# Two more batches' first layer in seven block products for eight, and 186 re-ranked operations, in a fused attention and MLP-mixer kernel

## The chip, the core and the metric

The kernel runs on one core of one Trainium2 chip. The core has five engines with queues of their own: PE (TensorE, the matmuls; the loading of its weights is shown as PEld), DVE (VectorE), ACT (ScalarE), POOL (GpSimd, which here issues most DMAs) and SP (SyncE, which issues DMA transposes and stores). Each engine works off its queue in the order in which the program was written; semaphores hold an instruction until what it needs is done. Matmuls write to PSUM, which has eight banks of 128 x 512 fp32 here; DVE and ACT empty it.

The metric is the device time of one execution in microseconds (us), the median of three runs.

## The reference

Eight batches, eight heads, 576 positions, head size 64. Attention with a sliding window of 128 and a linear bias (ALiBi), then an MLP mixer: a token-mixing pair of layers over the positions and a channel pair over the 512 features.

```
scores = q @ k^T / 8 ;  bias = -slope[h] * |i - j| ;  only 0 <= i - j < 128
x = softmax(scores + bias) @ v                    # heads side by side: 8 x 576 x 512
h = relu(x^T @ w_tok1) @ w_tok2                   # 576 -> 256 -> 576
u = x + h^T
out = u + relu(u @ w_ch1) @ w_ch2                 # 512 -> 1536 -> 512
```

## The kernel before, in words

**Tiles and stages.** Batches are taken in pairs: four blocks of 128 positions of each batch, and one tail block that holds the last 64 positions of both, so nine blocks to a pair. For each batch `main(b)` is the channel pair of layers and `side(b + 1)` the attention and the token mixing of the next batch. The two are interleaved on all engines. What `side` leaves for `main` is `ub` (the sum u, positions by features) and `uT` (its transpose, features by positions), which from batch 3 on is made by DMA transposes that SP issues (L974).

**The first layer.** A chunk (`chunk`, L1460) is four matmuls of 128 x 512 into one bank, 128 hidden units for the batch's 512 positions; one relu by ACT (L1466) or DVE (L1467) empties the bank into `r2`. Twelve chunks make a batch. In batch 7 (`UNITS[7]` is 3) the layer is cut into three units instead (`unit`). Each unit does the work of four chunks as a 2 x 2 block product with seven products in place of eight (Strassen's scheme in Winograd's form). `halves` (L1323) makes four differences of `uT` once, and `hidden_sums` (L688) made the sums of the weights long before. A product (L1360) is four matmuls of 128 x 256 into one bank, half a chunk. Three banks serve a unit. The bank `y` takes products 1, 6, 7 and 4 one after the other, `w` takes 5 and 3, `z` takes 2. After products 1, 5 and 6 the bank is copied out as fp32 (`keep`, L1375, into the ring `ob`, which outputs use too). After 2, 3 and 7 the bank and a kept copy are added into `r2` (`join`, L1384) and a relu in place follows (L1386 on DVE or L1388 on ACT); after 4 a relu empties the bank (L1411). A product that goes on in a bank waits for the eviction before it. Beside it `tail_piece` (L1503) does the first layer of the tail block.

**The second layer** is done in seven products in all batches (`second`, L1637), over sums of the hidden layer that DVE makes (`second_sums`, L1485) in two halves, with evictions by DVE (L1608) and stores (L1620). The tail block follows (L1548, L1555).

**The attention of a block** is `scores` (L770), an exp by ACT (L785), a product with the mask by DVE (L795), `values` (L858), a reciprocal (L871) and a scaling (L874) by DVE. The token mixing is L905, L915, a relu (L923 on ACT, L924 on DVE), L948, L944 and the sum into `ub` by DVE (L966).

**What sets the order.** All of this is first collected as operations with an engine, a cost, a rank and what they need. `Plan.run` then goes through them by a clock of its own: on each engine the operation that can start first is taken, and among those ready together the one with the lowest rank. `Plan.emit` writes the program in the order of the starts found. Operations are numbered (`o.n`) in order of creation. An operation's `after` is the earliest start that the clock allows it. Neither rank nor `after` puts a wait into the program: they change only the order on each engine's queue, and which buffer and which of two engines an operation gets. POOL's operations keep an order of their own (`order`). An operation with `other` may go to a second engine. PSUM banks are a ring: `ONE` is the four banks 4 to 7, `ANY` all eight; `gated` holds a unit's banks to `ONE` until the last scores of the next batch's side work have been placed.

The constants that the change touches, and the loop of the first layer that reads `UNITS`:

```
SEEDS = [0] * 9
UNITS = [0, 0, 0, 0, 0, 0, 0, 3]
...
if u >= NHT // 4 - UNITS[b]:
    rk = unit(b, u, rank, uT, tt, r2)
else:
    for t in (2 * u, 2 * u + 1, 6 + 2 * u, 7 + 2 * u):
        rk = chunk(t)
```

Of the kernel before, what the change touches and what calls it, by code (L numbers as in the profile page):

```python
# [71 lines left out]
class Plan:  # L72
# [59 lines left out]

    def run(self):
        ops = self.ops
        dice = [random.Random(x) for x in SEEDS]
        for o in ops:
            if SEEDS[o.part]:
# [241 lines left out]
GROUPS = (((0, 1, 2, 3), 250),)  # L379
UORDER = (1, 5, 2, 6, 3, 7, 4)  # L380
UNIT_RANK = 0
UNIT_LATE = False
SECOND_LATE = False
GATE = True
BANKS = 8
ALIKE = 0
UNITS = [0, 0, 0, 0, 0, 0, 0, 3]
FILL = 60000.0
START = 4300.0
LATE = (1500.0, 2790.0)  # L390
# [26 lines left out]
def kernel(  # L417
# [244 lines left out]
    def weight_sums():  # L662
        lo, hi = slice(0, HN), slice(HN, DM)
        for g in range(2):
            a, z = slice(3 * g, 3 * g + 3), slice(HK + 3 * g, HK + 3 * g + 3)
            got = []
            for i, x, y in ((0, WC2[:, a, hi], WC2[:, a, lo]), (1, WC2[:, z, hi], WT[:, 0, a, :]),
                            (2, WC2[:, z, hi], WC2[:, a, hi]), (3, WC2[:, z, lo], WT[:, 1, a, :])):
                def go(i=i, x=x, y=y, a=a):
                    dve_.tensor_tensor(out=WT[:, i, a, :], in0=x, in1=y, op=ALU.subtract)  # L670
                needs = [lc2[3 * g]] if i == 0 else [lc2[3 * g], lc2[HK + 3 * g]] + ([got[i // 2]] if i % 2 else [])
                got.append(plan.op("DVE", 154 + 3 * HN / 1.92, go, RANKT + i, needs=needs))
            lt.append(got)
# [3 lines left out]
    def hidden_sums():  # L677
        for u in range(NHT // 4):
            up, dn = slice(2 * u * P, 2 * (u + 1) * P), slice(DCH // 2 + 2 * u * P, DCH // 2 + 2 * (u + 1) * P)
            x, y = slice(0, NCB // 2), slice(NCB // 2, NCB)  # L680
            own = slice(2 * u * P, 2 * (u + 1) * P)
            got = []
            for i, f, a, z in ((0, ALU.add, WC1[:, x, dn], WC1[:, y, dn]),
                               (1, ALU.subtract, WS[:, 0, :, own], WC1[:, x, up]),
                               (3, ALU.subtract, WC1[:, y, up], WS[:, 1, :, own]),
                               (2, ALU.subtract, WC1[:, x, up], WC1[:, x, dn])):
                def go(i=i, f=f, a=a, z=z, own=own):
                    dve_.tensor_tensor(out=WS[:, i, :, own], in0=a, in1=z, op=f)  # L688
                needs = [lc1[x] for x in (2 * u, 2 * u + 1, 6 + 2 * u, 7 + 2 * u)]
                needs += [got[-1]] if i in (1, 3) else []  # L690
                got.append(plan.op("DVE", 154 + 2 * 2 * P / 1.92, go, RANKS + i, needs=needs, after=SUMS_AT))
            ls.append({1: got[0], 2: got[1], 4: got[2], 3: got[3]})
# [12 lines left out]
    weight_sums()  # L705
    if any(UNITS):
        hidden_sums()
# [621 lines left out]
    def unit(b, u, rank, uT, tt, r2):  # L1329
# [24 lines left out]
        def product(m, bk, more=(), new=True):  # L1354
            l, r, ws, ts = L[m]

            def go():
                for c in range(2):
                    for cb in range(2):
# [6 lines left out]
                         **({"makes": bk} if new else {"adds": bk}))  # L1366
            if UNIT_LATE and new:
                marks["wait"].append(op)
            return rk

        def half_of(x):
            return x().rearrange("p (c n) -> p c n", c=2)

        def keep(e, bk, rk):
            return plan.op("ACT", 600, lambda: act_.copy(out=e()[:, :], in_=bk()[:, :]), rk + UNIT_RANK, makes=e, uses=[bk],  # L1375
                           other=("DVE", 690, lambda: dve_.tensor_copy(out=e()[:, :], in_=bk()[:, :])))

        def mark(op, rows):
            for t in range(rows.start, rows.stop):
                r2.parts.setdefault(t, []).append(op)  # L1380

        def join(e, bk, rows, cols, rk):
            o = lambda: r2()[:, rows, cols]
            add = plan.op("DVE", 690, lambda: dve_.tensor_tensor(out=o(), in0=half_of(bk), in1=half_of(e), op=ALU.add),  # L1384
                          rk + UNIT_RANK, uses=[bk, e], part=(r2, ("sum", rows.start, cols.start)))
            mark(plan.op("DVE", RELU, lambda: dve_.tensor_scalar(out=o(), in0=o(), scalar1=0.0, scalar2=None, op0=ALU.max),  # L1386
# [47 lines left out]
    def main(b, rank):  # L1434
# [76 lines left out]

        if not UNITS[b]:
            turn_ = [0, 1, 2, 6, 7, 8, 3, 4, 5, 9, 10, 11] if quick else list(range(NHT))
# [6 lines left out]
        else:  # L1520
            tt = halves(b, rank, uT)
            for u in range(NHT // 4):
                if u >= NHT // 4 - UNITS[b]:
                    rk = unit(b, u, rank, uT, tt, r2)
# [205 lines left out]
```

## Time and profile before

| | us |
|---|---|
| median of three runs | 276.57 (276.26 to 276.59) |
| the profiled execution | 276.21 |
| its span, first to last instruction | 274.2 |
| PE busy (matmuls) | 267.9 |
| PEld busy (weight loads) | 182.2 |
| DVE busy | 209.4 |
| ACT busy | 136.9 |
| POOL busy | 114.3 |

How to read it: the span is what the profile shows of one execution, and some 2 us lie around it in the time of that execution. Matmuls are pipelined and their ends are modelled, so PE's busy time counts overlapping matmuls once, and a matmul shown with 0.27 us occupies PE for less when others follow. A row of the chain of waits gives a run of matmuls its true length. "Idle before" in a group of instructions is the time in which their engine stood still just ahead of them, with what ended it. Groups are by line, engine, operation and tile; "128x512 bf16<-128x512 f32" is output and input, partitions by elements. In the timeline a row is a start, a length, engine, line, operation and count.

### The profile page before, as it was taken

The numbers are of one execution on the slowest core, as the hardware profiler recorded it, in microseconds if no ns is written. First come the engines' busy times: TensorE is split into PE (matmuls) and PEld (weight loads), VectorE is DVE, ScalarE is ACT, GpSimd is POOL, SyncE is SP. The second block draws the span as 40 slices with busy tenths as digits, with TensorE's granted clock in tenths as the row PEclk, the third lists the DMA queues.
The fourth block names the chain that finished last, engine by engine and source line by source line (L and its number), as shares of the span: only waits on it lengthen the run. The fifth ranks groups of instructions, "written<-read, shape, count | busy, mean of one in ns | idle before, by whom it ended". The sixth has DMA issues, their size and how long they took to land.

```text
span 274.2 us, 7149 instructions
## 1 busy us (share of the span) xinstructions
PE 267.9 (98%) x2896; PEld 182.2 (66%) x2896; DVE 209.4 (76%) x482; ACT 136.9 (50%) x221; POOL 114.3 (42%) x146
## 2 busy tenths in 40 slices
PE   8989999999999999999999999999999999999994
PEld 5767566676686656585658656486658655489983
DVE  7987699977997479675968469684969469697972
ACT  6963795326871396207930097206940087205500
POOL 8979796830496009600890009700850410022000
PEclk9999999999999999999999999999999999999999
DMA  8999999999999999979999939989995810143014
GB/s 201 178 175 181 166 159 182 155 157 197 157 118 141 199 161 103 154 119 199 192 151 136 211 127 89 150 119 214 181 142 91 229 42 2 28 108 116 2 41 151
DMA packets 160336, 38.57 MB, mean 141 GB/s; under 512 B 146544, under 2 KB 159472, under 8 KB 160304
## 3 DMA queue, kind: packets, MB, share of 16 engines
q0 software_dynamic: 109968, 19.64, 90.2%
q1 hardware_dynamic: 49104, 17.70, 34.3%
q10 hardware_dynamic: 1232, 0.79, 1.0%
q8 instruction: 22, 0.36, 0.6%
q14 instruction: 10, 0.08, 0.1%
HBM read 35.85 MB, written 9.44 MB: 165 GB/s over the span
## 4 chain that ended last, share of the span: by engine, by line
PE 92%; DMA 4%; ACT 1%; issue 1%; POOL 0%; DVE 0%; POOLq 0%
PE ps L1637 27%; PE ps L1460 26%; PE ps L858 6%; PE ps L770 5%; PE ps L905 4%; PE ps L948 4%; PE ps L1503 4%; PE ps L1548 4%; PE ps L1360 3%; DMA W<-in_moe_w_tok_dram 2%; DMA v<-in_v_dram 2%; PE ps L1446 1%; PE ps L733 1%; PE ps L915 1%; PE ps L944 1%; PE ps L983 1%
## 5 line engine op out<-in xcount | busy, mean ns | idle before, releaser
L1466 ACT ACTIVATE r<-ps 128x512 bf16<-128x512 f32 x73 | 43.3, 600 | 76.1 <-PE ps L1460 68.9
L1460 PE MATMUL ps<-uT,WC 128*128 128x512 bf16 x324 | 78.7, 379 | 0.0
L579 POOL DMA_DIRECT2D v<-in_v_dram x36 | 30.6, 850 | 84.4 <-PE ps L858 81.8
L785 ACT ACTIVATE pe<-ps 128x1024 bf16<-128x1024 f32 (+1 forms) x56 | 50.9, 962 | 0.9 <-PE ps L770 0.8
L1460 PEld LDWEIGHTS <-WC 128*128 128x128 bf16 x324 | 29.1, 98 | 29.9 <-issue 1.1
L1637 PEld LDWEIGHTS <-r 128*128 128x128 bf16 x384 | 36.7, 98 | 6.7 <-issue 0.9
L579 POOL DMA_DIRECT2D qk<-in_q_dram x35 | 30.3, 869 | 4.0 <-DMA qkT<-qk 2.0
L579 POOL DMA_DIRECT2D qk<-in_k_dram x35 | 30.3, 871 | 3.7 <-DMA qk<-in_k_dram 1.3
L795 DVE TENSOR_TENSOR pe<-pe,mask 128x1024 bf16<-128x1024 bf16 (+1 forms) x48 | 30.4, 650 | 1.5 <-ACT pe L785 1.3
L1637 PEld LDWEIGHTS <-s 128*128 128x128 bf16 x288 | 27.7, 98 | 4.7 <-issue 1.0
L1637 PE MATMUL ps<-WC,r 128*128 128x256 bf16 x192 | 25.3, 273 | 0.0
L874 DVE TENSOR_TENSOR xb<-ps,rt 128x256 bf16<-128x256 f32 (+1 forms) x60 | 24.5, 419 | 0.7
L966 DVE TENSOR_TENSOR ub<-ps,xb 128x512 bf16<-128x512 f32 x32 | 19.8, 681 | 5.2 <-PE ps L948 5.2
L1637 PE MATMUL ps<-WT,r 128*128 128x256 bf16 x192 | 23.8, 273 | 0.0
L1637 PE MATMUL ps<-WT,s 128*128 128x256 bf16 x192 | 23.6, 273 | 0.0
L1608 DVE TENSOR_TENSOR raw<-ps,ub 128x512 f32<-128x512 f32 x27 | 18.2, 681 | 6.7 <-PE ps L1637 6.6
L858 PE MATMUL ps<-v,pe 128*128 128x65 bf16 (+1 forms) x480 | 21.9, 195 | 0.0
L858 PEld LDWEIGHTS <-pe 128*128 128x128 bf16 (+1 forms) x480 | 18.4, 99 | 5.2 <-DVE pe L795 1.1
L1620 POOL DMA_DIRECT2D out_dram<-raw x6 | 4.3, 718 | 37.0 <-DVE raw L1608 37.0
L770 PEld LDWEIGHTS <-qkT 64*128 64x128 bf16 x448 | 11.9, 94 | 8.9 <-issue 7.4
L1608 DVE TENSOR_TENSOR raw<-ps,raw 128x512 f32<-128x512 f32 x19 | 13.0, 688 | 5.9 <-PE ps L1637 5.9
L1467 DVE TENSOR_SCALAR r<-ps 128x512 bf16<-128x512 f32 x11 | 7.5, 686 | 11.1 <-PE ps L1460 8.9
(142 smaller groups left out, 400.0 us busy)
## 6 DMA issues: line engine op xcount, KB each, us to landing
out_dram<-raw SPq DMA_DIRECT2D x21, 256.0 KB, 3.5
qk<-in_q_dram POOLq DMA_DIRECT2D x30, 128.0 KB, 6.3
qk<-in_k_dram POOLq DMA_DIRECT2D x30, 128.0 KB, 6.1
v<-in_v_dram POOLq DMA_DIRECT2D x28, 128.0 KB, 6.1
WC<-in_moe_w_ch_dram POOLq DMA_DIRECT2D x8, 384.0 KB, 7.0
out_dram<-raw POOLq DMA_DIRECT2D x6, 256.0 KB, 3.4
v<-in_v_dram POOLq DMA_DIRECT2D x16, 64.0 KB, 4.8
out_dram<-ob SPq DMA_DIRECT2D x3, 256.0 KB, 2.7
```

Source lines behind the costliest of these rows:

```text
L579: nc.gpsimd.dma_start(out=to()[p0 : p0 + n, :, :], in_=rows(src, b, s0, n))
L770: pe_.matmul(wide(e)[:, i, kind, a:z], lhsT=ts[kb]()[e * D : (e + 1) * D, NHP + i, :], rhs=ts[blk]()[e * D : (e + 1) * D, i, a:z], start=T ...
L785: act_.activation(out=pb()[:, e, :, lo:, c0:c1_], in_=wide(e)[:, :, lo:, c0:c1_], func=ACT.Exp, scale=scale)
L795: dve_.tensor_tensor(out=o, in0=o, in1=heads(mk, es), op=ALU.mult)
L858: pe_.matmul(view()[a:z, at, i, :], lhsT=pb()[:, e, i, kind, a:z], rhs=vb()[:, h, 0 : D + 1], start=m == 0, stop=m == len(mms) - 1, skip_g ...
L874: dve_.tensor_tensor(out=x4(), in0=view()[r0:r1_, :, :, 0:D], in1=rt()[r0:r1_, 0:n, :, :].broadcast_to([r1_ - r0, n, 4, D]), op=ALU.mult)
L905: pe_.matmul(t1[j]()[:, :], lhsT=W1[:, blk % NC, j * P : (j + 1) * P], rhs=xb()[:, blk, :], start=c == 0, stop=False)
L966: plan.op("DVE", 690, lambda blk=blk, ht=ht, hs=hs: dve_.tensor_tensor(out=ub()[:, blk, :], in0=ht()[:, hs], in1=xb()[:, blk, :], op=ALU.a ...
L1460: pe_.matmul(ct()[:, :], lhsT=WC1[:, cb, t * P : (t + 1) * P], rhs=uT()[:, cb, :], start=cb == 0, stop=cb == NCB - 1)
L1466: plan.op("ACT", 600, lambda t=t, ct=ct: act_.activation(out=r2()[:, t, :], in_=ct()[:, :], func=ACT.Relu), rk, part=(r2, t), uses=[ct], o ...
L1608: dve_.tensor_tensor(out=v, in0=bk().rearrange("p (c n) -> p c n", c=2), in1=src, op=ALU.add)
L1637: pe_.matmul(bk()[:, c * HN : (c + 1) * HN], lhsT=l(t, c), rhs=w(t), start=first, stop=g == 1 and t == HK - 1, skip_group_check=True)
```

## The change

`UNITS` gets a 3 for batches 3 and 5, as batch 7 has it: all three units of their first layers are made of seven products instead of four chunks. Batches 3 and 5 are the second ones of their pairs, with a tail block, and the attention of batches 4 and 6 runs beside them. This adds 31 operations to each of the two batches, so later numbers in the order of creation move by 31 and then 62, to 1463 operations in all.

Before the plan runs, a new table `NUDGES` adds a number to the rank of 186 operations and gives 108 of them a floor for their start on the planner's clock, in nanoseconds. 89 of them are on PE, 59 on DVE, 23 on ACT, 13 on SP and 2 on POOL; 58 stand in the opening and the first two batches. Operation 274 is the copy of the last quarter of batch 0's `uT` (L1252); 908 is a DMA transpose of batch 4's `ub` (L974); 1457 is the second quarter of the very last output piece (L1548). Of the table the first and the last line are shown, and one from the part of batch 3.

```diff
     def run(self):
         ops = self.ops
+        for item in NUDGES.split():
+            n, rank, after = item.split(":")
+            ops[int(n)].rank += float(rank)
+            ops[int(n)].after = max(ops[int(n)].after, float(after))
         dice = [random.Random(x) for x in SEEDS]
...
 UNIT_RANK = 0
+NUDGES = ("12:-413:10740 15:-584:0 94:12660:106875 180:-624:7624 186:-377:7996 192:249:0 200:-876:14352 203:991:11015 "
...
+          "761:-670:131162 763:-1726:129980 765:3407:134943 766:4821:138150 769:7217:135329 771:-17678:0 778:12399:0 "
...
+          "1424:-8640:0 1428:8959:0 1429:6857:0 1442:11650:0 1457:8055:268226 ")
 UNIT_LATE = False
...
-UNITS = [0, 0, 0, 0, 0, 0, 0, 3]
+UNITS = [0, 0, 0, 3, 0, 3, 0, 3]
```

The lines with the operations that the prediction names:

```diff
+          "247:-100:16202 250:-701:21012 258:-958:22351 264:1004:21827 274:-158:26502 277:5057:33779 285:2619:27844 "
...
+          "859:12978:132589 861:-3784:131883 868:-6245:133680 885:-2813:0 889:3606:0 894:2453:0 908:8907:151484 "
```

21 rows, old and new, of the table NUDGES are left out of this document.

## The prediction

> **What bounds the kernel now.** I read the page's shares first, then the chain of work that ended last, then a table of busy time by stretch. In the last, each row is a stretch, its length, and then the busy time of PE, PEld, DVE, ACT and POOL with instruction counts, the granted clock, the DMA share and GB/s.
>
> ```profile
> PE 267.9 (98%) x2896; PEld 182.2 (66%) x2896; DVE 209.4 (76%) x482; ACT 136.9 (50%) x221; POOL 114.3 (42%) x146
> ...
> PE 92%; DMA 4%; ACT 1%; issue 1%; POOL 0%; DVE 0%; POOLq 0%
> ```
>
> ```profile
> 0.00:30.00 30.00, 27.41 (x416) 20.06 (x416) 24.16 (x77) 19.37 (x36) 26.22 (x38) 1.00 1.56 184
> 30.00:112.00 82.00, 82.00 (x895) 52.85 (x894) 67.57 (x155) 49.48 (x83) 44.73 (x55) 1.00 1.71 157
> ...
> 121.00:145.00 24.00, 24.00 (x279) 14.60 (x277) 16.51 (x39) 15.20 (x22) 13.68 (x16) 1.00 1.58 175
> 145.00:156.00 11.00, 11.00 (x94) 8.81 (x92) 6.96 (x12) 0.60 (x1) 0.00 (x0) 1.00 1.56 190
> ...
> 183.50:207.60 24.10, 24.10 (x280) 14.70 (x278) 16.75 (x39) 15.20 (x22) 9.27 (x11) 1.00 1.49 167
> 207.60:219.00 11.40, 11.40 (x94) 8.87 (x92) 7.02 (x13) 0.60 (x1) 2.88 (x4) 1.00 0.67 175
> ```
>
> From 30 us on PE is busy in every stretch without a gap, at full clock, and the chain that ends last lies on it for 92%. The first layer of batch 3 fills 121 to 145 us together with the attention of batch 4; its second layer follows to 156. Batch 5 has the same picture at 183.5 and 207.6. So PE sets the pace, and in the dense part a new order alone has nothing to win: there is no PE idle time to remove. It can only lose. Only less PE work, or a better opening, can shorten the kernel.
>
> **The PE work that goes.** Two rows of the chain of waits (start, length, what) give both forms, a run of eight first-layer matmuls (two chunks, L1460) and a run of 28 half-width matmuls (seven products, L1360) in batch 7:
>
> ```profile
> 129.55 1.73 PE ps L1460 x8
> ...
> 249.98 3.06 PE ps L1360 x28
> ```
>
> A chunk is 1.73/2 = 0.865 us, twelve are 10.38 us. Three units of seven products are 3 x 3.06 = 9.18 us. Each changed batch loses 1.20 us of PE time, both together 2.40 us. Since PE has no gaps there, all of it counts, unless a wait takes its place.
>
> **The vector work that comes.** The groups of batch 7's first layer and of batch 3's as it is (busy, mean ns of one):
>
> ```profile
> L1384 DVE TENSOR_TENSOR r<-ps,raw 128x512 bf16<-128x512 f32 x8 | 5.5, 690 | 1.2 <-PE ps L1360 1.0
> L1375 ACT COPY raw<-ps 128x512 f32<-128x512 f32 x8 | 4.5, 586 | 11.4 <-PE ps L1360 11.4
> L1386 DVE TENSOR_SCALAR r<-r 128x512 bf16<-128x512 bf16 x8 | 2.4, 294 | 0.3
> L1411 ACT ACTIVATE r<-ps 128x512 bf16<-128x512 f32 x3 | 1.8, 597 | 2.1 <-PE ps L1360 2.1
> L1388 ACT ACTIVATE r<-r 128x512 bf16<-128x512 bf16 x1 | 0.6, 622 | 0.0
> L1323 DVE TENSOR_TENSOR tt<-uT x2: 411/412/414, 243.7 to 244.1; 128x512 bf16<-128x512 bf16 x2
> L1323 DVE TENSOR_TENSOR tt<-uT,tt x2: 416/416/416, 244.4 to 245.6; 128x512 bf16<-128x512 bf16 x2
> ```
>
> ```profile
> L1466 ACT ACTIVATE r<-ps 128x512 bf16<-128x512 f32 x11 | 6.5, 599 | 15.4 <-PE ps L1460 12.1 <-DVE xt L898 3.3
> ...
> 126.68 0.69 DVE L1467 TENSOR_SCALAR r<-ps 128x512 bf16<-128x512 f32 x1 [2.56 <-PE ps L1460]
> ```
>
> A batch has twelve chunk evictions now, eleven on ACT and one on DVE. In their place come 9 keeps (ACT), 9 joins that add a bank and a kept copy (DVE), 9 relus after them (DVE, or ACT at 0.622), 3 last relus (ACT) and 4 differences of the transposed input (DVE). For DVE in batch 3's stretch: 16.51 - 0.69 + 9 x 0.690 + 9 x 0.294 + 2 x 0.412 + 2 x 0.416 = 26.34 us, in a stretch that is to last 24.00 - 1.20 = 22.80 us. That is 3.54 us too much. ACT: 15.20 - 11 x 0.599 + 9 x 0.586 + 3 x 0.597 = 15.67 us, so 7.13 us are idle. If ACT takes all nine relus (5.60 us), DVE has 26.34 - 2.65 = 23.69 us and is still 0.89 us short. For batch 5 (16.75 in 24.10) the same sums give 3.68 and 1.03 us.
>
> What is short in the stretch must be worked off in the next, where DVE has 11.00 - 6.96 = 4.04 us idle (batch 5: 4.38). That hides it only if what is put off is not what PE wants next. PE wants two things next: the sums of the hidden layer (L1485), which stand behind the joins in DVE's queue, and the token mixing of the next batch (L905, L948), which stands behind that batch's masks and norms. The exposed part lies between 0 (all of it put off into idle time) and 3.54 + 3.68 = 7.22 us (none). I take the shortage that is left after the best split of the two engines, 0.89 + 1.03 = **1.92 us**: it is nearest to a schedule that uses the free ACT, and both engines would still be 98% busy, which queues worked off in order hardly beat.
>
> A sentence of the Trainium skill speaks against this change: "TensorEngine Tiling (Array Packing)", section "PSUM Bottleneck", says that a faster TensorE does not make the emptying of PSUM faster, so that the copies may become the bottleneck, and that both ScalarE and VectorE should do them. It speaks of another way to speed up TensorE, but the 24 instructions above that come for 12 have that shape; read strictly it would give the time of the vector rival below.
>
> **The waits that come.** In a unit one bank takes products 1, 6, 7 and 4 in turn, and each but the first waits for the eviction of the one before: behind the waiting matmul stands all of PE's queue. In batch 7 nothing competes on DVE; in batches 3 and 5 a join can stand behind a mask or two norms of the next batch:
>
> ```profile
> L795 DVE TENSOR_TENSOR pe<-pe,mask 128x1024 bf16<-128x1024 bf16 x6 | 4.0, 683 | 0.0
> ...
> L874 DVE TENSOR_TENSOR xb<-ps,rt 128x256 bf16<-128x256 f32 x8 | 3.4, 420 | 0.1
> ```
>
> One such step late costs PE 0.42 to 0.68 us unless another batch's matmuls are put between; that is a part of the 1.92, not beside it. Until the last scores of the side work have gone out, the units' banks are held to the four that the values, tail pieces and transposes use too.
>
> **The re-ranked operations.** By creation order 89 are PE's, 59 DVE's, 23 ACT's, 13 SP's and 2 POOL's. A floor (third number) shapes the order that is written out, and the chip does not wait for it. POOL keeps its own order, so the two loads stay where they are. On SP transposes and stores change places:
>
> ```profile
> 143.75 5.71 SPq L974 DMA_TRANSPOSE uT<-ub  x4
> ...
> 206.17 5.12 SPq L974 DMA_TRANSPOSE uT<-ub  x4
> ```
>
> ```profile
> uT<-ub SPq DMA_TRANSPOSE x20, 2.4
> ```
>
> ```profile
> 156.29 0.86 PE ps L1460 x4
> ...
> 218.71 0.86 PE ps L1460 x4
> ```
>
> Batch 4's four transposes are issued by 149.46, the last lands 2.4 us later at about 151.9, and the first layer that needs them starts at 156.29: 4.4 us to spare (batch 6: 213.7 against 218.71, 5.0). That is the cover for a token mixing that is put off; with PE 1.20 us earlier, 3.2 to 3.8 us are left.
>
> In the opening DVE makes the last quarter of the first transposed input just ahead of the matmuls that need it, and PE has a gap shortly before:
>
> ```profile
> 26.32 0.42 DVE L1252 COPY uT<-ps 128x512 bf16<-128x512 bf16 x1 [0.38 <-PE ps L1249]
> ```
>
> ```profile
> 17.43 0.67 PE L1178 MATMUL ps<-v,pe 128*64 128x65 bf16 x16 [0.47 <-ACT pe L1072]
> ...
> 26.12 1.24 PE L1446 MATMUL ps<-uT,WC 128*128 128x512 bf16 x5
> ```
>
> That copy (operation 274) is among the re-ranked, with a floor. One instruction of its size let in ahead of it costs 0.42 us; a better order could close the 0.47 us gap. Ends -0.47 and +0.42; I take +0.21, half of the loss, since the floors on this part put things back rather than forward.
>
> **The sum.** The profiled execution took 276.21 us (span 274.2, 2.0 around it). 276.21 - 2.40 + 1.92 + 0.21 = 275.94. The three runs' median, 276.57, lies 0.36 above the profiled one, so 276.30 on its scale. **Forecast: 276.3 us**, no change that can be told: a measurement tells 0.2%, here 276.02 to 277.12, from none. With every unknown at its good end it is 276.57 - 2.40 - 0.47 = 273.7, at its bad end 276.57 - 2.40 + 7.22 + 0.42 = 281.8.
>
> **Rivals.**
> B1, the gain stays: shortage wholly put off into the idle DVE time of the second layers. For it: 4.04 and 4.38 us are more than 3.54 and 3.68, and ACT stands idle for 10 us there. Against: the sums must come first. 276.57 - 2.40 + 0.21 = 274.4 us.
> B2, half of it stays, one batch hides and the other does not: 276.57 - 2.40 + 0.96 + 0.21 = 275.3 us.
> C, slower: DVE becomes the bound in the two stretches. Place: the joins' queue. As in batch 7, DVE keeps eight relus of nine, so it is 3.54 - 0.29 + 3.68 - 0.29 = 6.64 us short; the second layers, where it is idle 37% of the time, take 37% of that, and 63%, 4.18 us, stop PE. 276.57 - 2.40 + 4.18 + 0.21 = 278.6 us. It decides once more than 1.1 us a batch is exposed. For it: 26 us of work in 23; against: ACT's 7.13 idle us.
> D, the next batch's transposed input comes late: the mixing of batch 4 is what is put off, and one of its transposes has a floor of 151.484 where the trace issues the first at 143.75. If that one alone goes last, its 5.71/4 = 1.43 us and 2.4 to land end at 155.3, against 155.1 wanted: 0.2 us. If all four follow it, 151.5 + 5.71 + 2.4 = 159.6, 4.5 us late. Middle 2.3: 276.57 - 2.40 + 2.3 + 0.21 = 276.7 us.
> E, PE was not the bound, so nothing is won: then 276.57 plus the opening's 0.42 = 277.0 us. The full rows of PE and the chain's 92% speak against it. The Trainium skill, "Perfetto Trace Analysis", section "Identifying the Most-Contended Engine", would have it so: it says that matmul busy time misleads and weight-load busy time is the better measure. Here that is 66%, below DVE's 76%; the trace's chain does not agree.
>
> **How the numbers follow.** A 0.28 (of it 0.03 faster, 0.22 same, 0.03 slower), B1 0.20, B2 0.13, C 0.22, D 0.10 (half same, half slower), E 0.07 (0.03 same, 0.04 slower). A is the forecast, its own range 275.8 to 277.3. Faster: 0.03 + 0.20 + 0.13 = 0.36; same: 0.22 + 0.05 + 0.03 = 0.30; slower: 0.03 + 0.22 + 0.05 + 0.04 = 0.34. The range reaches from just under B1 to C, 274.3 to 278.6, and leaves out some 0.08 below and 0.10 above.
>
> **What would show it.** PE's matmul time on L1460 falls by 24 chunks and L1360 rises to 252 matmuls with 7 in 3.06 us; if not, the first term is wrong. The rows of the two first-layer stretches should show DVE above 95% busy and PE, for the first time after 30 us, with gaps before L1360 or L1637 released by DVE, near 2 us in all. No gaps there means B1; gaps of 4 us or more, C; a gap before batch 4's or 6's first L1460 released by the transposes, D. The last uT copy of the opening should start within half a microsecond of 26.32. Wrong altogether would be gaps in stretches whose work is unchanged.

## The result and the profile after

The changed kernel takes 275.53 us (median of 22 runs, 274.17 to 278.4) against 276.71 us for the kernel before (22 runs, 276.11 to 277.74): a ratio of 0.9955, 95% interval 0.9941 to 0.997. It is faster by 0.45%, 1.2 us, half of the 2.4 us of PE work taken out. The prediction said 276.3 us and no change that can be told. Executions far above the others of their kernel (278.4 us here, one in e2, two each in e8 and e10, one in e11) count in the medians given below but not in the ratios and intervals, and the profiles of e2 and e11 are of such executions; without them the medians of e2, e8, e10 and e11 are 276.36, 275.64, 275.64 and 275.41 us.

Line numbers: behind L384 a line of the kernel before stands 30 lines further down in the changed kernel (L1360 is L1390, L1384 is L1414), and 5 lines further down in the variants that keep only a part of the table.

The page of the changed kernel, the shares and the chain that ended last:

```profile
PE 264.7 (96%) x2939; PEld 189.7 (69%) x2969; DVE 222.4 (81%) x514; ACT 142.9 (52%) x221; POOL 114.6 (42%) x146
...
PE 85%; DMA 5%; issue 2%; ACT 2%; POOL 2%; DVE 2%; POOLq 0%; ACTq 0%
```

This execution took 276.43 us (span 274.6), 0.9 above its kernel's median, and 30 matmul records are missing in it. The same kernel was profiled twice more; run e10 (275.62 us, span 273.9) lies near the median and has all 2969 matmuls, so the stretches and groups are shown from there. Busy time by stretch (columns as in the prediction):

```profile
30.00:112.00 82.00, 81.27 (x886) 52.24 (x881) 67.15 (x156) 49.24 (x75) 44.17 (x54) 1.00 1.73 156
...
121.00:145.00 24.00, 23.72 (x326) 19.12 (x324) 22.84 (x55) 17.72 (x27) 13.31 (x16) 1.00 1.50 170
145.00:156.00 11.00, 11.00 (x81) 7.68 (x80) 8.52 (x15) 1.04 (x3) 0.33 (x1) 1.00 1.51 171
...
183.50:207.60 24.10, 24.10 (x329) 19.46 (x328) 23.13 (x56) 16.86 (x25) 9.27 (x11) 1.00 1.43 165
...
247.00:260.00 13.00, 12.52 (x127) 11.06 (x125) 10.55 (x23) 9.76 (x18) 1.32 (x2) 1.00 0.22 75
```

DVE is busy for 22.84 of 24.00 and 23.13 of 24.10 us in the two stretches of the changed first layers, 95 and 96%, as predicted. PE, however, stands still there for only 0.28 us in the first and not at all in the second. Most of the 0.28 is this wait in PE's timeline, for a transpose of queries and keys and not for DVE:

```profile
124.33 0.23 PE L800 MATMUL ps<-qkT 64*128 64x128 bf16 x2 [0.24 <-DMA qkT<-qk]
```

The larger gaps are in stretches whose work is unchanged: 0.48 us from 247 to 260 us, batch 7, and 0.73 us from 30 to 112 us, of which 0.43 are a wait for a load of batch 1's keys and 0.29 one for a reciprocal by DVE.

The groups of the first layer by line (busy, mean ns, idle before), e10 again:

```profile
L1490 PE MATMUL ps<-uT,WC 128*128 128x512 bf16 x228 | 55.0, 379 | 0.0
...
L1414 DVE TENSOR_TENSOR r<-ps,raw 128x512 bf16<-128x512 f32 x25 | 16.8, 683 | 1.7 <-PE ps L1390 1.1 <-ACT raw L1405 0.4
L1390 PE MATMUL ps<-tt,WS 128*128 128x256 bf16 x108 | 15.9, 273 | 0.0
...
L1390 PE MATMUL ps<-uT,WC 128*128 128x256 bf16 x72 | 10.3, 273 | 0.0
...
L1418 ACT ACTIVATE r<-r 128x512 bf16<-128x512 bf16 x11 | 6.8, 633 | 3.2 <-DVE r L1414 3.2
L1390 PE MATMUL ps<-uT,WS 128*128 128x256 bf16 x36 | 5.4, 272 | 0.5 <-ACT raw L1405 0.2 <-DVE raw L1406 0.2
L1390 PE MATMUL ps<-tt,WC 128*128 128x256 bf16 x36 | 5.4, 272 | 0.0
L1416 DVE TENSOR_SCALAR r<-r 128x512 bf16<-128x512 bf16 x16 | 5.3, 332 | 0.2
```

The products are 108 + 72 + 36 + 36 = 252 matmuls, the chunks 228, as forecast. Of the 27 relus behind the joins ACT takes 11 and DVE 16.

**Where PE's time goes, by stretch.** Idle time alone does not show it, since PE also gets slower between its matmuls. So this is worked out from the traces: at each time, the time gone less the work of all matmuls started by then, each line's matmul at its usual spacing in the kernel before. What this lost time is above that of the profiled execution of before, in us, by the stretch in which it arises. Most traces lack some 30 matmul records, so a cell is good to about 0.2 us (0.3 in the first column):

| kernel (run) | 0-60 | 60-120 | 120-150 | 150-180 | 180-215 | 215-245 | 245-258 | all |
|---|---|---|---|---|---|---|---|---|
| changed, first profile | 1.38 | -0.11 | 0.34 | 0.10 | 0.33 | 0.00 | 0.82 | 2.86 |
| changed (e4) | 0.08 | 0.00 | 0.35 | 0.09 | 0.22 | 0.10 | 1.01 | 1.84 |
| changed (e10) | 0.25 | 0.00 | 0.65 | 0.04 | 0.21 | 0.15 | 0.81 | 2.11 |
| units without the table (e1) | 0.97 | 0.00 | 1.19 | 0.00 | 1.73 | 0.00 | 0.00 | 3.90 |
| the same, 18 relus left out (e7) | 3.05 | -0.12 | 1.08 | 0.00 | 2.09 | 0.00 | 0.00 | 6.11 |
| changed, 18 relus left out (e8) | -0.25 | 0.00 | 0.08 | 0.11 | 0.22 | -0.01 | 0.90 | 1.05 |
| table without batch 7 (e3) | 1.95 | 0.00 | 0.35 | 0.09 | 0.23 | 0.10 | 0.05 | 2.78 |
| the same again (e9) | -0.02 | 0.00 | 0.58 | 0.01 | 0.22 | 0.10 | 0.98 | 1.86 |
| table's middle alone (e6) | 2.58 | 0.16 | 1.62 | -0.42 | 1.14 | 0.00 | 0.00 | 5.09 |
| before with the early entries (e5) | -0.25 | 0.00 | 0.27 | 0.00 | 0.00 | 0.00 | 0.00 | 0.01 |
| before, other stores (e12) | 0.70 | 0.00 | 0.00 | 0.00 | 0.51 | 0.00 | 0.00 | 1.21 |

The units kernels have 2.42 us less work in the same reckoning, so e10's last matmul should start 2.42 - 2.11 = 0.31 us earlier than before's; it starts at 269.90 against 270.27, 0.37 earlier. Three things are to be seen. The two changed first layers (120-150 and 180-215) lose 0.57 and 0.86 us with the table (e4 and e10) and 2.92 us without it (e1). Batch 7 loses 0.8 to 1.0 in five of the six profiles with the early and middle entries, all but e3's. And the opening differs by more than 1 us between executions of one and the same order.

### The profile page after: what moved, and what is told of

The parts are those of the page before. It is cut to its first block, busy times and chain, and to the rows that moved or that the text cites. A ratio compares the mean times of both kernels' runs of the same rounds, so it can differ in the third digit from the quotient of the medians.

```text
span 274.6 us, 7275 instructions
## 1 busy us (share of the span) xinstructions
PE 264.7 (96%) x2939; PEld 189.7 (69%) x2969; DVE 222.4 (81%) x514; ACT 142.9 (52%) x221; POOL 114.6 (42%) x146
## 4 chain that ended last, share of the span: by engine, by line
PE 85%; DMA 5%; issue 2%; ACT 2%; POOL 2%; DVE 2%; POOLq 0%; ACTq 0%
PE ps L1667 27%; PE ps L1490 16%; PE ps L1390 9%; PE ps L888 6%; PE ps L800 5%; PE ps L978 4%; PE ps L935 4%; PE ps L1578 4%; DMA qk<-in_k_dram 3%; PE ps L1533 3%; DMA out_dram<-raw 2%; PE ps L1725 1%; PE ps L1051 1%; PE ps L945 1%; PE ps L1077 1%
## 5 line engine op out<-in xcount | busy, mean ns | idle before, releaser
L1490 PE MATMUL ps<-uT,WC 128*128 128x512 bf16 x212 | 53.5, 379 | 0.8 <-issue 0.2
L1496 ACT ACTIVATE r<-ps 128x512 bf16<-128x512 f32 x55 | 32.2, 600 | 34.4 <-PE ps L1490 32.5
L1490 PEld LDWEIGHTS <-WC 128*128 128x128 bf16 x228 | 20.5, 98 | 20.2 <-issue 0.2
L1405 ACT COPY raw<-ps 128x512 f32<-128x512 f32 x23 | 13.1, 593 | 27.0 <-PE ps L1390 26.0
L904 DVE TENSOR_TENSOR xb<-ps,rt 128x256 bf16<-128x256 f32 (+1 forms) x63 | 25.6, 416 | 0.7
L1667 PE MATMUL ps<-WT,s 128*128 128x256 bf16 x192 | 24.9, 273 | 0.0
L888 PEld LDWEIGHTS <-pe 128*128 128x128 bf16 (+1 forms) x480 | 19.9, 99 | 6.6 <-issue 0.6
L888 PE MATMUL ps<-v,pe 128*128 128x65 bf16 (+1 forms) x480 | 23.4, 194 | 0.5 <-DVE rt L901 0.3
L1638 DVE TENSOR_TENSOR raw<-ps,raw 128x512 f32<-128x512 f32 x20 | 13.7, 686 | 6.2 <-PE ps L1667 6.0
L1414 DVE TENSOR_TENSOR r<-ps,raw 128x512 bf16<-128x512 f32 x25 | 16.7, 682 | 1.7 <-PE ps L1390 1.1
```

The source lines that it names most:

```text
L888: pe_.matmul(view()[a:z, at, i, :], lhsT=pb()[:, e, i, kind, a:z], rhs=vb()[:, h, 0 : D + 1], start=m == 0, stop=m == len(mms) - 1, skip_g ...
L904: dve_.tensor_tensor(out=x4(), in0=view()[r0:r1_, :, :, 0:D], in1=rt()[r0:r1_, 0:n, :, :].broadcast_to([r1_ - r0, n, 4, D]), op=ALU.mult)
L1490: pe_.matmul(ct()[:, :], lhsT=WC1[:, cb, t * P : (t + 1) * P], rhs=uT()[:, cb, :], start=cb == 0, stop=cb == NCB - 1)
L1496: plan.op("ACT", 600, lambda t=t, ct=ct: act_.activation(out=r2()[:, t, :], in_=ct()[:, :], func=ACT.Relu), rk, part=(r2, t), uses=[ct], o ...
L1638: dve_.tensor_tensor(out=v, in0=bk().rearrange("p (c n) -> p c n", c=2), in1=src, op=ALU.add)
L1667: pe_.matmul(bk()[:, c * HN : (c + 1) * HN], lhsT=l(t, c), rhs=w(t), start=first, stop=g == 1 and t == HK - 1, skip_group_check=True)
```

## The experiments

### Units and table apart

e1 is the change of `UNITS` alone, no table. e2 is the changed kernel without the 57 entries with numbers below 602, which lie in the opening and the first two batches, e3 without those of batch 7 (1354 and above). e5 is the kernel before with the 57 early entries alone; e6 has the units and the entries from 602 to 1353.

```diff
-UNITS = [0, 0, 0, 0, 0, 0, 0, 3]
+UNITS = [0, 0, 0, 3, 0, 3, 0, 3]
```

> The units in batches 3 and 5 without the table of ranks and floors. Theory 1 (the vector work of the units is nearly hidden; the changed kernel loses about 1.3 us elsewhere, in the opening and at batch 7's first units): the opening and the end stay as before, so most of the 2.40 us is seen, about 274.8 us. Theory 2 (the prediction's: the vector shortage in the two stretches costs about 1.9 us, and the table only moves it): 276.2 to 277.5 us, with PE gaps released by DVE inside the two first layers.

> The changed kernel without the 57 entries of the table for operations below 602 (opening and first two batches). Theory 1: the opening is that of before and the transposes of batch 1's q and k do not wait for their loads, about 1 us less than the changed kernel, 274.5 us. Theory 2: the opening's entries cost nothing, the waits there are scatter of the loads, 275.5 us as with the whole table.

> The changed kernel without the entries for batch 7's main part (operations from 1354 on). Theory 1, the part about batch 7: if the order there makes the kept copies wait for output stores, the wait of about 1 us goes and the time is 274.5 us; if the wait comes from batch 6 ending earlier against the same stores, it stays and the time is 275.5 us. Theory 2: 275.5 us.

> The kernel before with the 57 early entries of the table alone (operations below 602), no new units. If the early entries are worth what the run without them lacked against the whole table (about 1 us): 275.8 us against 276.8. If that difference was scatter of the opening's loads: 276.8 us, no change.

> Units in 3, 5 and 7 with the entries 602 to 1353 alone: neither the early ones nor batch 7's. If only the middle matters: 275.2 us, as without batch 7's entries. If the early entries are worth 1 us: 276.2 us.

| run | median us | ratio to before | interval |
|---|---|---|---|
| e1, units alone | 277.42 | 1.0036 | 1.0015 to 1.0057 |
| e2, no early entries | 276.52 | 0.9985 | 0.9957 to 1.0014 |
| e3, no entries of batch 7 | 275.19 | 0.9943 | 0.992 to 0.9966 |
| e5, early entries alone | 276.73 | 1.0005 | 0.9979 to 1.0031 |
| e6, middle alone | 276.71 | 0.9987 | 0.9956 to 1.0019 |

The units alone make the kernel slower, though they take 2.4 us of work from the engine that bounds it; with the table they make it faster, and the intervals are apart (e4 below is the changed kernel in e1's session: 0.9939 to 0.9988). The table's early entries without the units do nothing; its other entries were not run without the units. What the units lose without it, the chain of e1 shows (start, length, what), in batch 3:

```profile
131.45 0.65 PE ps L770 x16
132.10 1.93 ACT pe L785 x2
134.02 1.04 ACT r L1388 x2
135.06 0.50 ACT r2t L1508
...
135.60 0.40 PE ps L858 x8
```

and the timeline of PE, with the waits in brackets:

```profile
133.74 1.05 PE L1503 MATMUL ps<-uTt,WC 128*128 128x128 bf16 x16 [0.19 <-DVE r L1384]
135.60 0.40 PE L858 MATMUL ps<-v,pe 128*128 128x65 bf16 x8 [0.24 <-ACT r2t L1508]
```

PE waits for banks: values (L858) and the tail piece (L1503) want one of the four banks that the unit shares with them, and a join (L1384) or the tail's relu (L1508) has yet to empty it. Those stand in their engines' queues behind two exps (L785) and two relus (L1388). The same rows come again at 196 to 198.5 us. In e10's timeline of these stretches no wait of PE on a join, a relu or an exp reaches 0.15 us. That is not for want of vector work. The two stretches in e1 (PE, PEld, DVE, ACT, POOL as above):

```profile
121.00:145.00 24.00, 23.26 (x313) 18.43 (x314) 22.17 (x52) 20.37 (x39) 13.08 (x16) 1.00 1.41 159
...
183.50:207.60 24.10, 22.98 (x309) 18.10 (x310) 22.08 (x52) 20.16 (x38) 9.25 (x11) 1.00 1.49 164
```

DVE is busy for 22.17 and 22.08 us, less than with the table (22.84 and 23.13), and PE stands still for 0.74 and 1.12 us. What differs is the order. Which entries do it, those of PE's own queue or those of DVE and ACT, no run separates.

e6 shows a second kind. From its chain of waits in batch 3:

```profile
119.91 4.30 DMA uT<-ub
```

and PE's timeline there:

```profile
125.41 1.47 PE L1642 MATMUL ps<-WT,r 128*128 128x256 bf16 x12 [1.12 <-DVE raw L1613]
```

and DVE's:

```profile
124.33 0.43 DVE L1328 TENSOR_TENSOR tt<-uT 128x512 bf16<-128x512 bf16 x1 [1.82 <-DMA uT<-ub]
124.67 0.68 DVE L1613 TENSOR_TENSOR raw<-ps,raw 128x512 f32<-128x512 f32 x1
```

The differences (`halves`, L1328 here) stand at the head of DVE's queue and wait for a transpose that takes 4.30 us to land. Behind them stands an eviction of batch 2's second layer (L1613) that PE waits for. DVE is not short of time there, it stands idle for 1.82 us in front of the first difference, and PE loses 1.12 us. In e10 the same eviction stands ahead of the differences (DVE's timeline):

```profile
120.73 0.69 DVE L1638 TENSOR_TENSOR raw<-ps,raw 128x512 f32<-128x512 f32 x1 [0.72 <-PE ps L1667]
121.82 0.43 DVE L1353 TENSOR_TENSOR tt<-uT 128x512 bf16<-128x512 bf16 x1 [0.39 <-DMA uT<-ub]
```

With the units in, the early entries seem to be worth 0.3 to 0.4% (e2 against the changed kernel, e6 against e3), but the intervals of both pairs overlap. The table of lost time shows a place: e6 loses 2.76 us in the two first layers, e3, with the same entries for the middle and the early ones besides, 0.58. Without the early entries the planner reaches batch 3 by another path and writes another order there. That is one profile of each; how much of it the times hold stays open.

### Are the relus the shortage?

e7 is e1, and e8 the changed kernel, with the 18 relus behind the joins of batches 3 and 5 left out, so part of the hidden layer keeps its negative values and the time is that of 18 vector instructions less. The queues are the same otherwise.

```diff
-    lambda: dve_.tensor_scalar(out=o(), in0=o(), scalar1=0.0, scalar2=None, op0=ALU.max)
+    lambda: b == B - 1 and dve_.tensor_scalar(out=o(), in0=o(), scalar1=0.0, scalar2=None, op0=ALU.max)
...
-    other=("ACT", 600, lambda: act_.activation(out=o(), in_=o(), func=ACT.Relu))
+    other=("ACT", 600, lambda: b == B - 1 and act_.activation(out=o(), in_=o(), func=ACT.Relu))
```

> The units without the table, and the 18 relus after the joins of batches 3 and 5 left out (the order of all else is unchanged, the output is not the reference's). Theory 2 in the form that the first runs leave (without the table the vector queues hold PE up, some 1.2 us in batch 3 and 1.7 us in batch 5): with the relus gone from ACT's and DVE's queues at least 2 of these 2.9 us go, 277.4 to about 275.2 us, and the ACT relus vanish from the chain at 132 to 136 us. Rival: PE waits for the four banks that the units hold, whatever the vector engines do, and the time stays at 277 us or more.

> The changed kernel with the same 18 relus left out (the order of all else is unchanged, the output is not the reference's). If the table has already hidden the vector work, little is left to win: 275.5 to 274.9 us, at most 0.7 us. If a shortage near the predicted 1.92 us is still exposed: 273.7 us.

e7 takes 277.3 us (1.0026, 1.0 to 1.0053), e8 275.93 us (0.9957, 0.9933 to 0.9981): neither can be told from its twin with the relus. A shortage of vector time would have shrunk by the 18 relus (in e1 ten on DVE and eight on ACT), each at least 0.20 us from start to start (rows further down), 3.6 us of one engine or the other; but e7's two first layers lose 3.17 us of PE time against 2.92 in e1. The chain of e7 says why:

```profile
132.77 0.60 DVE pe L795
...
133.46 0.67 DVE pe L795
134.13 0.33 DVE xb L874
134.46 1.21 DVE r L1384 x2
...
135.71 1.07 PE ps L1503 x16
```

The two joins that free the banks (L1384) still stand behind two masks and a norm of the next batch. The queue's order sets the wait, and taking the relus out of it did not bring these joins forward enough. The rival of e7's expectation, that PE waits for the four shared banks whatever the vector engines do, fits its time too. e10 speaks against "whatever": with the same four banks and more work on DVE it loses 0.86 us where e1 loses 2.92. No run gave the units more banks. In e8 the two first layers lose 0.30 us against 0.57 and 0.86 in e4 and e10, so 0.3 to 0.6 us seem to hang on the relus once the order is right, below what the times can tell.

### The 0.8 to 1.0 us in batch 7

Chain and POOL's timeline of e10, each in its own fence:

```profile
246.89 4.90 DMA out_dram<-raw
...
251.82 0.70 DVE raw L1406
...
252.56 0.61 PE ps L1390 x4
...
253.19 0.60 ACT raw L1405
```

```profile
245.44 0.74 POOL L1650 DMA_DIRECT2D out_dram<-raw  x1 [24.80 <-DVE raw L1638]
246.18 0.72 POOL L1650 DMA_DIRECT2D out_dram<-ob  x1
246.89 1.48 POOL L1650 DMA_DIRECT2D out_dram<-raw  x2
```

The kept copies of batch 7's units (L1405, L1406) take their buffers from the ring that batch 6's output pieces are stored from. Four stores of 256 KB are issued within 2.2 us; the first two land in 2.6 and 2.7 us, the third takes 4.90, DVE's copy starts 0.02 us after that, and PE's next product in that bank after the copy. The prediction has no such wait.

e3 leaves the table's entries of batch 7 out, and its profile showed no such wait, which looked like the answer. e4 and e10 are the changed kernel again, e9 is e3 again, e9 and e10 beside each other.

```diff
-NUDGES = (... "1346:9885:0 1351:-799:241808 1353:-12988:0 " ... "1457:8055:268226 ")
+NUDGES = (... "1346:9885:0 1351:-799:241808 1353:-12988:0 ")
```

> The changed kernel once more, for a second profile on the same chip as the others: 275.5 us; the wait on the stores at batch 7's first units should be there again (theory 1), the wait on the loads of batch 1's q and k may be shorter if it is scatter.

> The changed kernel without the table's entries of batch 7, timed again beside the changed kernel itself. If the wait on the output stores' buffers in batch 7 (0.8 to 0.95 us in the two profiles of the changed kernel) sets the end, this kernel is 0.6 to 1.0 us faster than the changed kernel in the same session, 274.4 to 274.9 us. If what follows that wait takes up the gap (the last stores, which both must wait for), the two agree within 0.3 us. The profile should show no wait of PE on the copies between 250 and 255 us.

> The changed kernel once more, as the other half of the comparison: 275.4 us, ratio 0.995 to 0.997, and again about 0.8 to 1.0 us of PE time lost between 245 and 255 us to copies that wait for output stores.

e4 takes 275.44 us (0.9964, 0.9939 to 0.9988), e9 275.8 us (0.9979, 0.9953 to 1.0006), e10 276.3 us (0.999, 0.996 to 1.0019). The changed kernel in three sessions: 0.9955, 0.9964, 0.999; the gain is of the size of its own scatter, and the third session alone would not show it. And e9 has the wait that e3, the same kernel, has not. ACT's timeline in e9, and then, from the view of the output pieces between 240 and 258 us, the time from issue to landing of three of the four stores in e9, e3 and before:

```profile
251.48 0.58 ACT L1380 COPY raw<-ps 128x512 f32<-128x512 f32 x1 [1.48 <-DMA out_dram<-raw]
```

```profile
DMA to landing us min/median/max: 2.6/4.7/4.9
```

```profile
DMA to landing us min/median/max: 2.6/3.0/3.3
```

```profile
DMA to landing us min/median/max: 2.6/2.6/3.2
```

So the entries of batch 7 are not the cause. In the five profiles in which the last two stores took 4.7 to 5.1 us (first profile, e4, e8, e9, e10) PE loses 0.8 to 1.0 us; in e3 and e6, where they took 3.0 to 3.4, at most 0.05. What goes with the late landing can be seen in the DMA view, from the third store to its landing or shortly after, in e9 (246.5 to 251.5 us):

```profile
q0 software_dynamic: 305, 0.99, 56.3%
q8 instruction: 1, 0.02, 1.5%
```

and in e3 (248.3 to 251.9 us):

```profile
q0 software_dynamic: 309, 1.01, 79.7%
```

q0 carries the stores. In each of the five a packet of 16 KB of the queue that the profile calls `instruction` starts 2.2 to 2.5 us after the third store was issued, while the stores are being written, and takes 1.1 to 1.5 us; the last seven of the 256 store packets of 4 KB then follow one at a time, 0.16 us or more apart, when the others are done. In e3 and e6 it starts 3.6 and 3.7 us after the third store, behind the last store packet. In the kernel before (and in e5 and e12) it falls on the first of the four stores, which takes 3.1 to 3.3 us where the others take 2.2 to 2.6, and PE loses nothing there. Seven packets are about what one of 16 DMA engines has of two stores (an estimate: 64 packets a store, 4 to an engine, 8 for two). So the delay looks like one DMA engine held up by that packet. No run moved the packet, the engine of a packet is not recorded, and why it starts at another time in e9 than in e3, the same program, is open.

e11 issues them from SP, everything else in the same order; e12 does so in the kernel before.

```diff
-            q_ = nc.gpsimd if late else nc.sync
+            q_ = nc.gpsimd if late and b != B - 2 else nc.sync
```

> The changed kernel, but batch 6's four stores of 256 KB are issued by SP instead of POOL; every other queue keeps its order. In five profiles of the table's order these stores took 4.7 to 5.1 us from issue to landing and PE lost 0.8 to 1.0 us between 245 and 255 us to copies that wait for them. If POOL's queue is what makes them slow, they land in about 2.7 us as SP's other stores of this size do, no copy waits for a store, PE loses under 0.2 us there, and the kernel is 0.7 to 1.0 us faster than the changed kernel: 274.5 to 275 us, ratio 0.992 to 0.994. If the four stores within 2.2 us are slow in any queue, landing stays at 4.5 us or more and the time stays at 275.4 to 276.3.

> The kernel before with the same four stores issued by SP. Its profile shows no wait on stores, so nothing is to be won: 276.5 to 276.9 us, ratio 0.998 to 1.002. A gain here like that of the changed kernel would say that the queue helps for another reason than the wait.

e11 takes 275.44 us (0.9949, 0.9927 to 0.9972), e12 277.17 us (1.0013, 0.9992 to 1.0034). e11's interval overlaps those of the changed kernel, so a gain is not shown, and its profile cannot tell how long the stores take to land. The Trainium skill, "DMA: Bandwidth & Descriptors", section "Issuing engines are not separate DMA queues", says that DMAs of all issuing engines end up on the same 16 DMA engines, so that another issuer saves little beyond the issue itself. e12's profile agrees: issued by SP, the last three of these stores land 2.18 to 2.20 us after the start of the issue, in the kernel before, issued by POOL, after 2.56 to 2.58, and POOL's issue itself is the longer one by about as much (0.72 against 0.37). The 274.5 to 275 us expected of e11 were missed by half a microsecond, the 276.5 to 276.9 of e12 by 0.3.

No variant beats the changed kernel by more than the intervals allow; e3 has the lowest median, 275.19 us, but not in its second run.

## Why the prediction was right or wrong

The forecast was 0.8 us too high: no change was called, 1.2 us of gain came. The range held it. That owes something to luck: a shortage taken too large and a wait that was not foreseen nearly made up for each other. The nearest rival is B2, half of the gain, at 275.3 us, though not by its mechanism.

**PE as the bound, and the work removed: right.** 96 chunk matmuls went and 168 half-width ones came, which the reckoning puts at 2.42 us against 2.40. That e1 is slower in spite of it is no sign that PE was not the bound (rival E): with the table the time does fall.

**"A new order alone has nothing to win; it can only lose": wrong as used.** It holds for the kernel before as far as it was tried (e5: 1.0005). But the prediction carried it over to the kernel with units, where e1 shows 2.9 us of waits that come from order. Without the table there is no gain: 277.42 us in e1 against 275.44 in e4, in the same session.

**The vector shortage, +1.92: the step that failed, by its size and by what sets it.** With the table the two first layers lose 0.57 and 0.86 us (e4 and e10), without it 2.92 (e1), though DVE is busy for less time there. So the exposed part does not follow from a balance of DVE's time; the order of the queues sets it. The balance was also too high. The term priced each added DVE instruction at the whole length of its row. DVE's timeline in e10 shows what a full queue pays:

```profile
126.66 0.29 DVE L1416 TENSOR_SCALAR r<-r 128x512 bf16<-128x512 bf16 x1
126.86 0.69 DVE L1414 TENSOR_TENSOR r<-ps,raw 128x512 bf16<-128x512 f32 x1
127.52 0.69 DVE L825 TENSOR_TENSOR pe<-pe,mask 128x1024 bf16<-128x1024 bf16 x1
128.13 0.68 DVE L1414 TENSOR_TENSOR r<-ps,raw 128x512 bf16<-128x512 f32 x1
128.73 0.41 DVE L901 RECIPROCAL rt<-ps 128x4 f32<-128x4 f32 x2
```

From start to start a relu is 0.20 and not 0.29, a join 0.60 to 0.66 and not 0.69: one instruction begins some 0.08 us before the other's row ends. Of the prediction's split, with nine relus on ACT, twelve instructions more come to DVE in each batch; at 0.08 less each that is 1.0 us (an estimate), about the shortages of 0.89 and 1.03. Hardly any was left. DVE's whole account says the same: 30 of the 32 added instructions, priced by the mean of their rows, are 18 joins x 0.683 + 2 copies x 0.676 + 8 relus x 0.332 + 8 differences x 0.418 - 6 evictions x 0.686 = 15.5 us more, and DVE's busy time rose by 222.4 - 209.4 = 13.0. Part of the work was also put off, as rival B1 had it: in 145 to 156 us DVE goes from 6.96 to 8.52 us, and nothing waits. So 95% busy was right, and the conclusion that queues so full hardly work without gaps was not. (The "98% busy" of both engines is their mean: by the prediction's own sums DVE has 23.69 us of work in 22.80, ACT 21.27. And its "24 instructions that come for 12" are 34 in its own list, 21 of which empty a bank.) Rival C, DVE as the bound, did not come.

**The waits in the units, "a part of the 1.92": the mechanism right, its price set by the order.** Without the table they are what e1's chain shows in the two first layers, which lose more than the term (2.9 us); with it, 0.57 to 0.86 us are lost there, of which 0.24 in e10 are the wait for a transpose of queries and keys.

**The opening, +0.21 with bounds -0.47 and +0.42: not resolved, bounds too narrow.** The last copy of the first `uT` was to start within half a microsecond of 26.32. In the first profile's timeline of DVE it starts 0.99 earlier (in e4 and e10 0.96 and 0.98):

```profile
25.33 0.41 DVE L1282 COPY uT<-ps 128x512 bf16<-128x512 bf16 x1
```

That lead does not last. e5, which has the early entries alone, is 0.25 ahead at 60 us and level at 150. And the same order gives 1.38, 0.08 and 0.25 us in three executions. PE's timeline of the first and then of e10 shows a part of it:

```profile
28.62 0.40 PE L763 MATMUL ps<-ident,qk 128*128 128x128 bf16 x4 [0.54 <-DMA qk<-in_q_dram]
...
33.94 0.40 PE L763 MATMUL ps<-ident,qk 128*128 128x128 bf16 x4 [0.44 <-DMA qk<-in_k_dram]
```

```profile
32.92 0.40 PE L763 MATMUL ps<-ident,qk 128*128 128x128 bf16 x4 [0.43 <-DMA qk<-in_k_dram]
```

The loads of batch 1's queries and keys land at other times, and PE waits for them. From 60 to 120 us next to nothing is added.

**From the profile to the median, +0.36.** This was taken over to the changed kernel. Before's profiled execution (276.21) was a good one, 0.5 us under the median of its 22 runs, with an opening that e12, the same but for four stores at 245 us, does not have. The changed kernel's profiled executions took 276.43, 275.35 and 275.62 us, around its 275.53. Against them the forecast on the profiled scale, 275.94, was 0.5 too low once and 0.6 and 0.3 too high; the shift made it 0.8 too high against the median.

**Batch 7: missing.** The prediction called gaps in stretches whose work is unchanged the sign that it is wrong altogether. There is one, 0.8 to 1.0 us, by two stores that land late. It hid how far off the 1.92 was: e4 and e10 lose 1.77 and 1.86 us from 120 us on, close to the term by accident. Without that wait the time would be 275.53 less 0.8 to 1.0, about 274.6 (an estimate; no run shows it), near B1's 274.4, and the prediction's own sign, no gaps in the two first layers, names B1 too.

**The cover of the transposes: held.** (Rival D set a floor on the planner's clock beside times of the trace, which are two clocks.) Rival D did not come: no wait before batch 4's or 6's first chunk in e10, and 0.04 and 0.15 us lost in those stretches.

## What to carry to other kernels

When work on the bounding engine is swapped for work on the others, ask first not whether those have time but what stands ahead of the instruction that frees the bank: the same units cost PE 2.9 us or under 0.9 us, by the order of the queues. Price an instruction in a full queue from start to start, not by the length of its row. And profile a kernel more than once before half a microsecond is explained: one of two profiles of the same code had a wait of 1 us that the other had not.

## What the runs showed of the hardware

- Of four stores of 256 KB issued within 2.2 us the last two took 4.7 to 5.1 us to land in five profiles and 3.0 to 3.4 in two (e3, e6). In the five a 16 KB packet of the queue `instruction` ran while they were written, in the two after it. That the packet is the cause was not tested. Spread over 4.3 us, as in the kernel before, the stores took 2.6 to 3.2.
- DVE begins an instruction some 0.08 us before the row of the one ahead of it ends (the middle value over e10's rows that follow without a gap). So the rows of 30 added instructions sum to 15.5 us, and the busy time rose by 13.0.
- Executions of one program differ in the opening by more than a microsecond (PE's lost time up to 60 us: 0.08 to 1.38 for the changed kernel) and carry it to the end, since PE's rows from there on have hardly any idle time in which to catch up.
